# A fused attention and two-layer kernel: second layer's list by its places, conversions from slot 28 on, raw loads ahead of stores

## The chip, the cores and the metric

One core of one Trainium2 chip. The metric is device time in microseconds (us), the median of the timed runs. TensorE is called PE here, VectorE DVE, ScalarE ACT, GpSimd POOL, and SyncE, which issues all transfers of this kernel, SP.

## What is computed

Attention with a decay (no softmax) for 4 sequences of 576 tokens and 8 heads of 64, and then two feed-forward layers over the 2304 tokens. The weights come as 64-bit floats, which the chip must turn into pairs of 32-bit ones.

```python
def reference(q, k, v, moe_w_in, moe_w_out, moe2_w_in, moe2_w_out):
    # q, k, v: (4, 8, 576, 64); w_in: (512, 2048), w_out: (2048, 512), float64
    scores = q @ k.transpose(0, 1, 3, 2) / 8
    a = (scores * Dmat) @ v              # Dmat[h] = gamma_h ** (i - j) for i >= j, else 0
    x = a.transpose(0, 2, 1, 3).reshape(2304, 512)
    h = x @ moe_w_in
    x = (h * cos(h)) @ moe_w_out
    h = x @ moe2_w_in
    g = where(h >= 1, h, where(h <= -1, 0, (h + 1) ** 2 / 4))
    return g @ moe2_w_out
```

## The kernel before

**First layer.** Tokens go in five blocks (256 and then four times 512), the hidden units in 16 columns of 128. A *slot* is one block by one column; there are 80, those of blocks 0 and 1 mixed with each other (0 to 31), then 16 for each of blocks 2, 3 and 4. In slot s PE runs twelve matmuls `h<-xhl,wi` (L612) and the second twelve of slot s-2, `bky<-gh,wo` and `bky<-gl,wo` (L627 to L629). In between, h * cos(h) is made in turn by ACT (L662), DVE (L666), ACT (L670, L671), DVE (L675), ACT (`gh`, L683) and POOL (`gl`, L688): the high part `gh` and the low part `gl` of the result, since each matmul operand is kept as two parts. PE takes up the attention of a later block (L384) between slots, with steps on POOL (L370, L380), DVE (L472, L418, L519) and ACT.

The weight columns of block 0 and 1 are converted by these engines from the raw 64-bit words (loads `raw`, `rsh`), stored to `wd` and reloaded (`wi<-wd`, L314) three slots ahead of each use from block 2 on. Buffers for `wi` are a ring of five (pool `wr`).

**Background work.** The 32 matrices of the second layer (16 columns of each of two weights) are converted during the first layer. The list `bg` is spread over the slots from `bg0` to the sixth from the end. A matrix is loaded in its slot (`load_raw`, L200), begun one slot later (ACT, L226), and in the slot after that turned into 32-bit values on DVE (`W<-X` L239, `X<-W` L240, `X<-raw,X` L275, `V<-W,X` L276), split into parts `cw` (ACT L291, DVE L292) and stored (`wq<-cw`, `wv<-cw`, L294). With the second of a pair come sums and differences of the pair (DVE L300 to L302, parts `tw` on ACT L304, DVE L306, POOL L308, stores L310). `cw` takes its buffer from the ring of five of `wi`.

A scheduler sets the order of each engine from slot 24 on; ahead of that the opening's list does it.

**Second layer.** It computes its products in seven combinations of matrices each, over three token blocks of 768 and four steps of the hidden units: twelve units `n` of seven products (`bkT<-xc,w`, twelve matmuls each) and seven groups (`bkT<-gh,w`, `bkT<-gl,w`). Inputs are loaded from `yd` into four tiles `q` (`q<-yd`, four loads a token block), summed on DVE (`q<-q,q`), and split into `xc` parts 0 to 8 in turn (ACT rounds, DVE subtracts). Weights come in a ring of seven tiles `w`. Its steps are first written down as operations with an engine, a cost, a place in time `pos` and what they wait for; `listed()` then walks through them with a clock of its own and makes the order of each engine, which is kept as it is. The inputs of a later token block have places from 70 before it on, the weights 16 before their product; a unit has 28. Products 1, 6, 2, 5, 7, 4 and 3 of the first unit are mixed with the last two second halves of the first layer. Ahead of product 6 ACT copies bank T0 into T1 (`bkT1<-bkT0`, "the seed"), on which PE goes on adding up.

In `listed()` the time from which an operation may be placed was, for all, 60 ahead of the first product:

```python
ready = [-60.0] * len(ops)
free = dict(PE=0.0, ACT=-60.0, DVE=-60.0, POOL=-60.0, SP=-60.0)
```

Of the kernel before, what the change touches and what calls it, by code (L numbers as in the profile page):

```python
# [23 lines left out]
NC = DFF // P  # L24
# [86 lines left out]
def retention_moe_kernel(ctx: ExitStack, tc: tile.TileContext, qk, kv, win1, wout1, win2, wout2, ktab, out):  # L111
# [25 lines left out]
    V, A, G, SY, PE = [Ordered(e) for e in (nc.vector, nc.scalar, nc.gpsimd, nc.sync, nc.tensor)]  # L137
# [37 lines left out]
    def behind(later, earlier):  # L175
        tc.add_manual_dep(later.ins, earlier.ins.name, mybir.DependencyInfo(mybir.DependencyClass.NoSync, mybir.DependencyReason.SCHED_ONLY), reason="pace")
# [16 lines left out]
    def load_raw(L, i, c, homes=None):  # L193
        src = wsrc[L, i][c]
        twice = L == 0 and (i, c) not in ONCE
        tag = "raw" if twice else ("raw", "rsh")[turn[0] % 2] if L == 0 else ("raw", "raw", "rsh")[turn[0] % 3]
        turn[0] += not twice
        pool, first, second = (cv, tag, "rsh") if homes is None else (wp, *homes)
        t = pool.tile([P, DM, 2], I32, tag=first, name="raw")
        i0 = SY.dma_start(out=t, in_=src)  # L200
        if L == 1 and len(done) > 1:
            behind(i0, done[-2])
        t2 = None
        if twice:
            t2 = pool.tile([P, 4 * DM], I16, tag=second, name="rsh")
            SY.dma_start(out=t2[:, 1:], in_=src.rearrange("p n two -> p (n two)").bitcast(I16)[:, :4 * DM - 1])
        raws[L, i, c] = t, t2
# [47 lines left out]
    def begin(L, i, c, after=None):  # L255
        return Conversion(L, i, c, after).X()
# [3 lines left out]
    def home1(i, c):  # L260
        if i == 0:
            wi[0, c] = wr.tile([P, 2, DM], F32R, tag="wi", name="wi")
            return wi[0, c]
        wo[0, c] = wp.tile([P, 2, DM], F32R, tag=f"wo{c}", name=f"wo{c}")
        return wo[0, c]

    def store1(c):
        SY.dma_start(out=wd[c], in_=f(wi[0, c]))
# [43 lines left out]
    def load_wi(c):  # L312
        t = wr.tile([P, 2, DM], F32R, tag="wi", name="wi")
        SY.dma_start(out=f(t), in_=wd[c])  # L314
        wi[0, c] = t
# [283 lines left out]
    pos_of = {x: s for s, x in enumerate(slots)}  # L599
# [37 lines left out]
    def evac(s, home=None, only=None):  # L637
        l, c = slots[s]
        if c != NC - 1:
            return  # L640
        o, n = BLOCKS[l]
        per = 512 // n
        for e, y in enumerate(yb[l]):
            if only not in (None, e):
                continue
            t = stp.tile([P, 512], F32, tag="st", name="st") if home is None else home
            copy_out(e, t, y, -TWOPI)
            SY.dma_start(out=yd[:, e * per:(e + 1) * per, o:o + n], in_=t.rearrange("p (k n) -> p k n", k=per))
# [44 lines left out]
    def steps_of(s, which):  # L693
        for x in which:
            if (x, s) not in taken:
                taken.add((x, s))
                STEPS[x](s)
# [6 lines left out]
    def run_plan(pos):  # L704
        for fn in plan.pop(pos, []):
            fn()
# [141 lines left out]
    queue = [x for x in order if x not in loaded]  # L848
# [1 line left out]
        load_raw(0, *queue.pop(0))  # L850

    bg = [x for q in range(NQ) for x in ((0, q), (0, q + NQ), (1, q), (1, q + NQ))]
    bg0 = pos_of[1, NC - 1] + 2
    begun2 = {}
    per = (N1 - 6 - bg0) / len(bg)
    bgpos = {}
# [7 lines left out]
    def spill_2(i, c):  # L864
        spill(i, c, begun2.pop((i, c)))
        if c >= NQ:
            spill_sums(i, c - NQ)

    ops = []
# [99 lines left out]
    for s in range(N1):  # L969
        l, c = slots[s]  # L970
        if s == 24:
            by_hand[0] = 0
        run_plan(2 * s)
        steps_of(s, "m")
        if s >= 1:
            steps_of(s - 1, "CgG")
        steps_of(s, "haA")

        todo = [x for x in jobs.get(s, []) if x not in opened]
        begun = [begin(0, *x) for x in todo]  # L980
        for x in todo:
            begun.pop(0).rest(home1(*x))
            if x[0] == 0:
                store1(x[1])
            if queue:
                load_raw(0, *queue.pop(0))
        run_plan(2 * s + 1)
        if s >= LAG:
            steps_of(s - LAG, "M")
            evac(s - LAG)  # L990
        for x in bgpos.get(s - 2, []):
            spill_2(*x)
        for x in bgpos.get(s, []):
            load_raw(1, *x)
        steps_of(s, "b")
        for x in bgpos.get(s - 1, []):
            begun2[x] = begin(1, *x, after=mark[0])
        for c2 in reload.get(s, []):
            load_wi(c2)

        for fn in early.get(s, ()):
            fn()
# [217 lines left out]
    def listed():  # L1220
        waits = [len(o[4]) for o in ops]
        users = [[] for _ in ops]
        for n, o in enumerate(ops):
            for x, lands in o[4]:
                users[x].append((n, lands))
        ready = [-60.0] * len(ops)
        free = dict(PE=0.0, ACT=-60.0, DVE=-60.0, POOL=-60.0, SP=-60.0)
        queue = {e: {n for n, o in enumerate(ops) if o[0] == e and (e == "PE" or not waits[n])} for e in free}
        order = []
        while len(order) < len(ops):  # L1230
            best = None
            for e, ns in queue.items():
                if e == "PE":
                    n = min(ns, default=None)
                    if n is None or waits[n]:
                        continue
                elif ns:
                    t1 = min(max(free[e], ready[n]) for n in ns) + 0.15
                    n = min((n for n in ns if max(free[e], ready[n]) <= t1), key=lambda n: (ops[n][2], n))
                else:  # L1240
                    continue
                t = max(free[e], ready[n])
                if best is None or t < best[0]:
                    best = t, n
            t, n = best
            e, cost = ops[n][:2]
            queue[e].remove(n)
            free[e] = t + cost
            order.append((t, n))
            for u, lands in users[n]:  # L1250
                ready[u] = max(ready[u], t + cost + (0.0 if not lands or ops[u][0] == e else 6.0 if e == "SP" else 0.12))
                waits[u] -= 1
                if not waits[u] and ops[u][0] != "PE":
                    queue[ops[u][0]].add(u)
        return order

    order2 = listed()
    by_hand[0] = 1
    for _, n in order2:
# [103 lines left out]
```

## Time and profile before

| | |
|---|---|
| median of 3 timed runs | 835.67 us (834.68 to 838.59) |
| profiled execution | 838.97 us, span from first to last instruction 837.2 us |
| PE busy | 811.9 us, 97% |
| PE weight loads | 729.6 us, 87% |
| DVE busy | 642.5 us, 77% |
| ACT busy | 543.1 us, 65% |
| POOL busy | 166.9 us, 20% |
| granted PE clock, mean | 0.993 |
| moved by DMA | 232.92 MB, 278 GB/s |

Shares are of the span and average over stages with different limits: the first layer runs to about 470 us, the second from there to the end. A matmul's end is modelled, and matmuls overlap, so the distance from one start to the next says how fast PE goes. In a row of the timeline, "[4.81 <-ACT bkT L128]" is idle time of the engine ahead of that instruction and the step that ended it. L128 is the line of a helper that records whatever an ordered list issues; there the tile names tell the steps apart.

### The profile page before, as it was taken

The numbers are of one execution on the slowest core, as the hardware profiler recorded it, in microseconds if no ns is written. First come the engines' busy times: TensorE is split into PE (matmuls) and PEld (weight loads), VectorE is DVE, ScalarE is ACT, GpSimd is POOL, SyncE is SP. The second block draws the span as 40 slices with busy tenths as digits, with TensorE's granted clock in tenths as the row PEclk, the third lists the DMA queues.
The fourth block names the chain that finished last, engine by engine and source line by source line (L and its number), as shares of the span: only waits on it lengthen the run. The fifth ranks groups of instructions, "written<-read, shape, count | busy, mean of one in ns | idle before, by whom it ended". The sixth has DMA issues, their size and how long they took to land.

```text
span 837.2 us, 14788 instructions
## 1 busy us (share of the span) xinstructions
PE 811.9 (97%) x5549; PEld 729.6 (87%) x5550; DVE 642.5 (77%) x933; ACT 543.1 (65%) x893; POOL 166.9 (20%) x131
## 2 busy tenths in 40 slices
PE   8999899999999999999999799999999999999997
PEld 5788789888778677778777699999999999999997
DVE  7988878448898899888986548589786776874676
ACT  4778788754656554656666458678657786566672
POOL 2333223432334444234244100000000000000000
PEclk9999999999999999999999899999999999999999
DMA  9997999745888997687977478889897888898883
GB/s 351 379 386 267 352 326 324 263 154 182 300 299 312 328 340 293 237 278 278 362 286 252 151 276 250 253 255 322 255 327 253 254 251 254 263 319 250 256 253 136
DMA packets 78007, 232.92 MB, mean 278 GB/s; under 512 B 8304, under 2 KB 15088, under 8 KB 77936
## 3 DMA queue, kind: packets, MB, share of 16 engines
q1 hardware_dynamic: 77936, 231.98, 80.7%
q8 instruction: 44, 0.72, 0.3%
q14 instruction: 27, 0.22, 0.1%
HBM read 184.76 MB, written 47.19 MB: 277 GB/s over the span
## 4 chain that ended last, share of the span: by engine, by line
PE 43%; DVE 6%; DMA 3%; ACT 2%; issue 1%; SPq 0%; POOL 0%; DVEq 0%; ACTq 0%
PE bkT L128 41%; DMA wi<-wd 2%; DVE cw L292 1%; DVE t L666 1%; DVE X L275 1%; DMA wq<-cw 1%; DVE t L675 1%; DVE V L276 1%; DMA q<-yd 0%; PE bky L128 0%; DMA wv<-tw 0%; PE bky L629 0%; DMA wv<-cw 0%; PE bkO L612 0%; PE h L612 0%
## 5 line engine op out<-in xcount | busy, mean ns | idle before, releaser
L128 PE MATMUL bkT<-xc,w 128*128 128x384 f32 x1008 | 180.9, 337 | 4.8 <-ACT bkT L128 4.8
L128 PEld LDWEIGHTS bkT<-xc,w 128*128 128x128 f32 x1008 | 176.8, 189 | 5.6 <-ACT bkT L128 5.5
L128 PE MATMUL bkT<-gh,w 128*128 128x384 f32 x672 | 170.8, 335 | 0.3 <-ACT bkT L128 0.3
L612 PE MATMUL h<-xhl,wi 128*128 128x512 f32 (+1 forms) x576 | 139.3, 389 | 2.3 <-DVE t L675 2.3
L612 PEld LDWEIGHTS h<-xhl,wi 128*128 128x128 f32 x576 | 105.5, 188 | 26.1 <-DVE t L675 4.2
L128 PEld LDWEIGHTS bkT<-gh,w 128*128 128x128 f32 x672 | 121.2, 188 | 0.6 <-ACT bkT L128 0.6
L688 POOL TENSOR_TENSOR gl<-t,gh 128x512 fp32r<-128x512 f32 (+1 forms) x57 | 81.6, 1433 | 158.0 <-ACT gh L683 99.5
L128 PE MATMUL bkT<-gl,w 128*128 128x384 f32 x336 | 112.3, 334 | 0.0
L629 PE MATMUL bky<-gl,wo 128*128 128x512 f32 x208 | 78.6, 393 | 4.2 <-POOL gl L688 4.2
L627 PE MATMUL bky<-gh,wo 128*128 128x512 f32 x208 | 81.8, 394 | 0.0
L628 PE MATMUL bky<-gh,wo 128*128 128x512 f32 x208 | 81.1, 390 | 0.0
L683 ACT ACTIVATE gh<-t 128x512 fp32r<-128x512 f32 (+1 forms) x57 | 35.3, 619 | 53.9 <-DVE t L675 53.9
L128 PEld LDWEIGHTS bkT<-gl,w 128*128 128x128 f32 x336 | 63.1, 188 | 0.0
L128 DVE TENSOR_TENSOR gl<-a,gh 128x768 fp32r<-128x768 f32 x48 | 45.2, 953 | 14.0 <-ACT gh L128 14.0
L128 PE MATMUL h<-xhl,wi 128*128 128x256 f32 (+1 forms) x288 | 53.0, 335 | 2.7 <-ACT hs L128 2.7
L670 ACT ACTIVATE t<-t 128x512 f32<-128x512 f32 (+1 forms) x56 | 34.9, 623 | 31.3 <-DVE t L666 31.2
L128 DVE SCALAR_TENSOR_TENSOR a<-bkT,a 128x768 f32<-128x768 f32 x36 | 34.4, 956 | 26.2 <-ACT a L128 25.6
L128 PEld LDWEIGHTS h<-xhl,wi 128*128 128x128 f32 x288 | 44.6, 194 | 8.6 <-ACT hs L128 3.1
L629 PEld LDWEIGHTS bky<-gl,wo 128*128 128x128 f32 x208 | 38.8, 188 | 14.7 <-POOL gl L688 6.7
L128 DVE TENSOR_TENSOR a<-bkT,a 128x768 f32<-128x768 f32 (+1 forms) x46 | 43.0, 937 | 10.9 <-PE bkT L128 10.9
L627 PEld LDWEIGHTS bky<-gh,wo 128*128 128x128 f32 x208 | 39.0, 188 | 8.8 <-issue 0.5
L128 ACT ACTIVATE gh<-a 128x768 fp32r<-128x768 f32 x48 | 40.1, 836 | 8.8 <-PE bkT L128 8.4
(187 smaller groups left out, 1529.9 us busy)
## 6 DMA issues: line engine op xcount, KB each, us to landing
w<-wq SPq DMA_DIRECT2D x84, 512.0 KB, 4.5
w<-wv SPq DMA_DIRECT2D x84, 512.0 KB, 4.6
wi<-wd SPq DMA_DIRECT2D x48, 512.0 KB, 5.2
raw<-in_win_dram SPq DMA_DIRECT2D x32, 512.0 KB, 6.1
raw<-in_wout_dram SPq DMA_DIRECT2D x32, 512.0 KB, 5.4
qkv<-in_qk_dram SPq DMA_DIRECT2D x16, 512.0 KB, 7.0
qkv<-in_kv_dram SPq DMA_DIRECT2D x16, 512.0 KB, 8.5
wd<-wi SPq DMA_DIRECT2D x16, 512.0 KB, 6.3
```

Source lines behind the costliest of these rows:

```text
L128: ins = fn(*args, **kw)
L275: V.scalar_tensor_tensor(out=X, in0=raw[:, :, 0].bitcast(U32), scalar=2.0 ** -52, in1=X, op0=ALU.mult, op1=ALU.mult)
L276: done.append(V.tensor_tensor(out=v, in0=W, in1=X, op=ALU.add))
L292: V.tensor_tensor(out=t[:, ks, 1], in0=u, in1=f(t)[:, ks, 0], op=ALU.subtract)
L612: lastpe[0] = PE.matmul(hp[s][:, :n], w[:, a, kb, :], x[b][:, kb, :], start=(i == 0), stop=(i == 3 * KB - 1))
L627: PE.matmul(o, w[:, 0, es], a, start=first and e % per == 0, stop=False, skip_group_check=True)
L628: PE.matmul(o, w[:, 1, es], a, start=False, stop=False, skip_group_check=True)
L629: PE.matmul(o, w[:, 0, es], b, start=False, stop=last, skip_group_check=True)
L666: V.scalar_tensor_tensor(out=t, in0=t, scalar=-MAGIC, in1=h, op0=ALU.add, op1=ALU.subtract)
L670: A.activation(u, u, AF.Sin, scale=TWOPI / 2)
L683: A.activation(gh[s], rt[s], AF.Copy)
L688: G.tensor_tensor(out=gl[s], in0=u, in1=f(gh[s]), op=ALU.subtract)
```

## The change

Three edits. The background conversions begin at slot 28 (`pos_of[0, NC - 1] + 1`) instead of 33. In a slot that converts and stores a column of the first layer, the next raw loads are issued ahead of the stores. And in `listed()` an operation on SP, or one that waits for nothing, may be placed no earlier than its own `pos`; all others, and the engines PE, ACT, DVE and POOL, start at 0.

```diff
-    bg0 = pos_of[1, NC - 1] + 2
+    bg0 = pos_of[0, NC - 1] + 1
...
         for x in todo:
             begun.pop(0).rest(home1(*x))
+            if queue:
+                load_raw(0, *queue.pop(0))
+        for x in todo:
             if x[0] == 0:
                 store1(x[1])
-            if queue:
-                load_raw(0, *queue.pop(0))
...
-        ready = [-60.0] * len(ops)
-        free = dict(PE=0.0, ACT=-60.0, DVE=-60.0, POOL=-60.0, SP=-60.0)
+        ready = [o[2] if o[0] == "SP" or not o[4] else 0.0 for o in ops]
+        free = dict(PE=0.0, ACT=0.0, DVE=0.0, POOL=0.0, SP=-60.0)
```

In `ops`, `o[0]` is the engine, `o[2]` the place `pos` and `o[4]` the set of operations waited for.

ACT at the seam of the layers, from the last `gh` of the first layer on; xc5 and xc6 are inputs of the first token block, xc7 and xc8 of the second. Before:

```order
L683 ACTIVATE gh_5436<-t_5418 128x512
L128 ACTIVATE xc5_5483<-q2_4976 128x768
L128 ACTIVATE xc6_5498<-q3_4978 128x768
L128 ACTIVATE xc7_5481<-q0_4972 128x768
L128 ACTIVATE xc8_5482<-q4_5071 128x768
L128 ACTIVATE bkT1_5536<-bkT0_5511 128x2x384
L128 ACTIVATE u2_5480<-bkT1_5536 128x768
L128 ACTIVATE a1_5478<-bky0_4770 128x512
```

And now:

```order
L683 ACTIVATE gh_5436<-t_5418 128x512
L128 ACTIVATE bkT1_5518<-bkT0_5493 128x2x384
L128 ACTIVATE xc5_5534<-q2_4978 128x768
L128 ACTIVATE u2_5480<-bkT1_5518 128x768
L128 ACTIVATE xc6_5551<-q3_4980 128x768
L128 ACTIVATE a1_5478<-bky0_4793 128x512
```

The seed has moved ahead of the four roundings, and xc7 and xc8 have left this place.

DVE at the turn from blocks 0 and 1 to block 2, from the copy-out of block 0 (`st<-bkO`) on; `t<-t,hs` are the steps L666 and L675 of a slot of block 1. Before:

```order
L635 TENSOR_SCALAR st<-bkO 128x512
L666 SCALAR_TENSOR_TENSOR t<-t,hs 128x512
L675 SCALAR_TENSOR_TENSOR t<-t,hs 128x512
L666 SCALAR_TENSOR_TENSOR t<-t,hs 128x512
L675 SCALAR_TENSOR_TENSOR t<-t,hs 128x512
L666 SCALAR_TENSOR_TENSOR t<-t,hs 128x512
L675 SCALAR_TENSOR_TENSOR t<-t,hs 128x512
```

And now:

```order
L635 TENSOR_SCALAR st<-bkO 128x512
L666 SCALAR_TENSOR_TENSOR t<-t,hs 128x512
L239 TENSOR_SCALAR W<-X 128x512
L240 TENSOR_SCALAR X<-W 128x512
L275 SCALAR_TENSOR_TENSOR X<-raw,X 128x512
L675 SCALAR_TENSOR_TENSOR t<-t,hs 128x512
L276 TENSOR_TENSOR V<-W,X 128x512
L666 SCALAR_TENSOR_TENSOR t<-t,hs 128x512
L239 TENSOR_SCALAR W<-X 128x512
L240 TENSOR_SCALAR X<-W 128x512
L292 TENSOR_TENSOR cw<-V,cw 128x2x256
L275 SCALAR_TENSOR_TENSOR X<-raw,X 128x512
```

The steps of the conversions stand between L666 and L675 here already.

SP at the same turn, from the first reload `wi<-wd0` on; `wd0` to `wd4` are the columns that block 2 begins with. Before:

```order
L314 DMA wi_2306<-wd0_101 128x1024
L200 DMA raw_2670<-in_wout2_dram 128x1024
L364 DMA qkv_2246<-in_qk_dram 128x1024
L364 DMA qkv_2246<-in_kv_dram 128x1024
L314 DMA wi_2345<-wd1_102 128x1024
L314 DMA wi_2387<-wd2_103 128x1024
L364 DMA qkv_2347<-in_qk_dram 128x1024
L364 DMA qkv_2347<-in_kv_dram 128x1024
L648 DMA yd_100<-st_2298 128x2x256
L648 DMA yd_100<-st_2301 128x2x256
L314 DMA wi_2426<-wd3_104 128x1024
L314 DMA wi_2543<-wd4_105 128x1024
```

And now:

```order
L648 DMA yd_100<-st_2303 128x2x256
L314 DMA wi_2367<-wd1_102 128x1024
L294 DMA wq0_117<-cw_2355 128x512 x2
L200 DMA raw_2593<-in_win2_dram 128x1024
L314 DMA wi_2430<-wd2_103 128x1024
L294 DMA wq0_117<-cw_2411 128x512
L310 DMA wq0_117<-tw_2418 128x512 x4
L200 DMA raw_2476<-in_wout2_dram 128x1024
L294 DMA wv0_121<-cw_2472 128x512
L314 DMA wi_2480<-wd3_104 128x1024
L314 DMA wi_2600<-wd4_105 128x1024
```

The reloads of block 2 have spills and raw loads between them now, and `wd1` has moved behind both stores of block 0.

## Rows read from the trace of the kernel before

**Rows 1.** The page, part 1: busy time, share of the span, instructions.

```profile
PE 811.9 (97%) x5549; PEld 729.6 (87%) x5550; DVE 642.5 (77%) x933; ACT 543.1 (65%) x893; POOL 166.9 (20%) x131
```

**Rows 2.** Busy time by stage: stretch, length, engines, PE clock, DMA share, GB/s.

```profile
163.00:191.00 28.00, 28.00 (x223) 22.82 (x223) 12.82 (x22) 15.53 (x27) 9.17 (x7) 1.00 0.56 189
191.00:260.00 69.00, 68.83 (x585) 55.26 (x584) 59.60 (x104) 40.44 (x74) 24.68 (x20) 1.00 0.78 269
260.00:355.00 95.00, 92.00 (x767) 73.57 (x766) 85.46 (x135) 54.66 (x95) 36.91 (x26) 1.00 0.84 300
355.00:455.00 100.00, 95.40 (x412) 76.43 (x412) 86.78 (x126) 62.38 (x108) 37.81 (x25) 1.00 0.84 299
```

**Rows 3.** Timeline of PE at the seam: start, length, instruction, count, idle before.

```profile
469.35 2.24 PE L128 MATMUL bkT<-xc,w 128*128 128x384 f32 x12
471.43 0.62 PE L128 MATMUL bky<-gh,wo 128*128 128x512 f32 x2
...
473.93 0.39 PE L128 MATMUL bky<-gl,wo 128*128 128x512 f32 x1
479.13 4.21 PE L128 MATMUL bkT<-xc,w 128*128 128x384 f32 x12 [4.81 <-ACT bkT L128]
483.14 1.00 PE L128 MATMUL bky<-gh,wo 128*128 128x512 f32 x2
...
486.25 14.07 PE L128 MATMUL bkT<-xc,w 128*128 128x384 f32 x80
```

**Rows 4.** Busy time by stage, behind the seam and deep in layer two.

```profile
479.10:483.10 4.00, 3.97 (x12) 3.97 (x13) 2.10 (x3) 0.00 (x0) 0.00 (x0) 0.50 0.01 2
...
520.00:800.00 280.00, 280.00 (x1615) 280.00 (x1615) 202.15 (x224) 190.93 (x239) 0.00 (x0) 1.00 0.84 270
```

**Rows 5.** Timelines of ACT and DVE at the seam.

```profile
477.54 0.84 ACT L128 ACTIVATE xc<-q 128x768 fp32r<-128x768 f32 x1 [2.28 <-DVE q L128]
478.29 0.79 ACT L128 ACTIVATE bkT<-bkT 128x768 f32<-128x768 f32 x1
...
476.55 1.95 DVE L128 TENSOR_TENSOR q<-q,q 128x768 f32<-128x768 f32 x2 [2.51 <-DMA q<-yd]
```

**Rows 6.** Timeline of SP at the seam.

```profile
467.23 7.19 SPq L128 DMA_DIRECT2D q<-yd  x4
```

**Rows 7.** Timeline of PE, three of its ten idle times from 260 to 455.

```profile
278.56 0.50 PE L629 MATMUL bky<-gl,wo 128*128 128x512 f32 x1 [1.51 <-POOL gl L688]
...
372.54 3.04 PE L612 MATMUL h<-xhl,wi 128*128 128x512 f32 x12 [0.99 <-DVE t L675]
...
452.21 1.19 PE L629 MATMUL bky<-gl,wo 128*128 128x512 f32 x4 [0.75 <-POOL gl L688]
```

**Rows 8.** Groups of DVE by line and form, 190 to 460: busy, mean ns, idle.

```profile
L275 DVE SCALAR_TENSOR_TENSOR X<-raw,X 128x512 f32<-128x512 uint32 x32 | 25.7, 804 | 0.7
...
L301 DVE TENSOR_TENSOR V<-V 128x256 f32<-128x256 f32 x16 | 6.8, 423 | 0.5
```

**Rows 9.** Timeline of DVE, first step of a conversion.

```profile
191.40 1.49 DVE L239 TENSOR_SCALAR W<-X 128x512 int32<-128x512 int32 x1
```

**Rows 10.** Third token block's inputs: SP's timeline, busy time by stage.

```profile
563.19 0.37 SPq L128 DMA_DIRECT2D q<-yd  x1
...
570.00:580.00 10.00, 10.00 (x59) 10.00 (x59) 8.98 (x11) 8.21 (x11) 0.00 (x0) 1.00 1.01 379
```

**Rows 11.** Waits of SP's queue (us, times, longest), and landing of reloads.

```profile
SPq L294 <- DVE cw L292: 52.6, 21, 5.5
...
SPq L314 <- DMA wq<-cw: 14.3, 4, 7.0
...
wi<-wd SPq DMA_DIRECT2D x48, 512.0 KB, 5.2
```

**Rows 12.** POOL: timeline near the seam; group by form, 190 to 460.

```profile
466.23 1.29 POOL L688 TENSOR_TENSOR gl<-t,gh 128x512 fp32r<-128x512 f32 x1 [2.63 <-ACT gh L683]
...
L688 POOL TENSOR_TENSOR gl<-t,gh 128x512 fp32r<-128x512 f32 x43 | 64.3, 1497 | 122.9 <-ACT gh L683 78.3 <-issue 41.9 <-PE bky L629 1.9
```

## Prediction

> **What bounds the kernel now.** I read the busy line of the page first: PE is busy 811.9 of 837.2 us [rows 1], so whatever the other engines do, the time can fall only where PE stands still or runs at a lower clock. The busy time by stage then tells where that is. From 191 to 260 us PE loses 0.17 us in all; from 260 to 455 us it loses 3.00 + 4.60 = 7.60 us [rows 2]; from 520 to 800 us, deep in the second layer, nothing, at the full clock [rows 4]. Third, the timeline of PE around the seam between the layers: behind the matmul at 473.93 us it is idle for 4.81 us, released by ACT's `bkT` [rows 3]. So there are two sorts of loss: one hole at the seam, and ten small ones while the first layer's last blocks run, most of them put down to DVE's L675 or to POOL's `gl` behind it [rows 7]. The opening up to 100 us has losses too, but the two orders agree there row by row.
>
> The hole at the seam is read from three engines. ACT's step that PE waits for is the seed, a copy of bank T0 into T1, at 478.29 us; its input is there once the first product is through, a little after PE goes on to its next work at 471.43 us [rows 3]. It comes so late because ACT's row has four xc roundings ahead of it, and the last, at 477.54, waited 2.28 us for DVE's `q` at 476.55, which waited 2.51 us for a load q<-yd [rows 5]. That load is one of the four of the *second* token block, issued from 467.23 us on [rows 6]; PE needs nothing of them in the first four units of products.
>
> **The list of the second layer.** The new starting times keep a load from being planned before its place, and ACT and DVE from being planned before zero. In ACT's new order the seed comes first, with xc7 and xc8 more than forty rows further down; PE's order from the first product on is the same in both. What goes, start to start: the product behind the hole began at 479.13 and would begin when the twelve matmuls ahead of it end, 473.93 + 0.23 = 474.16: 4.97 us. Its own twelve matmuls took 483.14 - 479.13 = 4.01 us, where the first product's took 471.43 - 469.35 = 2.08: 1.93 us, and the twelve behind it 486.25 - 483.14 = 3.11 where the twelve from 471.43 took 474.16 - 471.43 = 2.73: 0.38 us [rows 3]. These two are the clock: granted 0.50 (1.2 of 2.4 GHz) from 479.1 to 483.1 us, after the engine had stood idle [rows 4]. Sum 4.97 + 1.93 + 0.38 = 7.28, **7.3 us**.
>
> What is late next? The seed can begin when the first product is done, by 471.7, takes 0.79 [rows 5] and ends at 472.5, 1.7 us before PE wants it. The four loads that stood ahead of the weights now stand behind 23 weight loads, whose ring of seven reaches 7 x 2.08 = 14.6 us ahead of PE. That loads do no harm there is seen on those of the third token block, which already lie between weight loads at 563.19 us: PE was busy 10.00 of the 10.00 us from 570, with the DMA engines full [rows 10]. So they cost nothing while the ring is full; without that cover one late weight, a product's length of 2 us. Bounds of the part: 7.6 to 5 us.
>
> **Conversions from slot 28 on.** 32 matrices are still converted, the last still from slot 72 on, so nothing is removed; 41 slots become 46 (1.28 and 1.44 slots a matrix). On DVE ten groups of steps do this, 162.6 us in all or 5.1 us a matrix, from 25.7 us (L275) down to 6.8 us (L301) [rows 8]. A slot is 24 matmuls of 0.227 us, 5.44 us; of these the conversions take 5.1 / 1.28 = 4.0 us now and 5.1 / 1.44 = 3.5 us then. DVE as a whole is busy 85.46 + 86.78 of 195 us, 88% [rows 2]; 0.5 us less in each slot makes it 79%. The new place has room: from 163 to 191 us DVE was busy 12.82 of 28 us and the DMA engines 56% [rows 2], and the first conversion began at 191.40 us [rows 9]; five slots earlier is 164. Five slots take 3.5 matrices, 18 us, and 12.82 + 18 = 31 is a little more than the 28 there are, so I don't count on this stretch staying without holes. At 59.60 of 69 us PE lost 0.17 us, between 191 and 260 [rows 2].
>
> What this saves is not in the rows, so I bound it. At best the holes shrink to what the stretch from 191 to 260 us shows, 0.17 in 69 or 0.5 in 195: a gain of 7. At worst the new stretch pays the 3 us that don't fit, the old holes stay, and as the order within a slot changes everywhere, one more of the largest kind comes in (1.51 us [rows 7]): a loss of 4.5. I take a gain of **2 us**, between the ends and nearer to no gain: with the trace's durations laid on DVE's order, twelve slots hold more than 5.44 us of steps between two L675 now and nine then, so a quarter of 7.6 should go.
>
> **Raw loads ahead of stores.** SP's order is the same row for row up to the first reloads of block 2, and all slots with such stores lie ahead of that. So the edit moves no instruction, **0 us** either way: not the text but the scheduler sets the place there. If a load did move, its cover would be the two raw tiles already filled.
>
> **Sum.** 7.3 + 2 + 0 = 9.3 us. Against the profiled execution, 838.97 us (span 837.2 and 1.8 around it), that is 829.7; it was 3.3 us over the median of the timed runs, 835.67, so for the median the forecast is **826.4 us**. With the bounds: 835.67 - 7.6 - 7 = 821.1 to 835.67 - 5 + 4.5 = 835.2, both ends unlikely together.
>
> **Rivals.** First, *the small holes stay or move forward*: the conversions press by their order in DVE's queue, not by their share of it. For it: a hole of 0.75 us came even at 452 us [rows 7], among the last conversions, whose place stays. Time 835.67 - 7.3 = 828.4, up to 832.9 with the loss of 4.5.
>
> Second, *the list does not do what it says*: the seed comes early but PE meets another late step right behind it, the banks that DVE and ACT empty for the fourth product, or a weight behind the stores of those banks. Against it: these steps follow PE's own matmuls, as they do now. If the whole hole only shifted: 835.67 - 2 = 833.7.
>
> Third, *POOL and DVE hold each other up in the moved slots*. POOL's `gl` takes 1.29 us where no conversion runs (466.23) and 1.50 in the mean among them [rows 12]. At worst DVE would stand for a whole `gl` in each moved slot, 5 x 1.3 = 6.5 us: 826.4 + 6.5 = 832.9. Against it stands the 0.17 us lost from 191 to 260, with the same instructions side by side. The Trainium skill's page "SBUF — State Buffer", section "SBUF: two separate sides", has a rule that speaks for this rival: VectorE operations with two SBUF inputs and GpSimd operations share a port pair, and the one that starts first holds it for its whole instruction. The longer mean agrees with it in direction; that PE lost almost nothing says that such a block stays inside the slack.
>
> Fourth, **slower than before**: the spills now stand in SP's queue between the first reloads of block 2, and their `cw` tiles come from the ring of five that the reloads use. SP has waited up to 5.5 us for DVE's `cw`, and a reload up to 7.0 us for a `cw` store to leave its buffer; a reload lands in 5.2 us [rows 11]. Together that is 17.7 us, against a lead of three slots, 16.3; beyond that PE stands still. Two holes like the one at the seam, 7.1 us each with the clock, make 826.4 + 14.2 = 840.6. Against it: after 191 us the same queue does this without a PE wait for a reload.
>
> **Chances.** Forecast 0.64 (822.5 to 828.4), small holes stay 0.18, list without effect 0.08, POOL against DVE 0.04, late reloads 0.06. About 0.5% (4.2 us, so 831.5 and 839.9) is what a measurement of this kernel can tell from no change. The first rival lies below 831.5 for two thirds, 0.12: faster 0.64 + 0.12 = 0.76, same 0.06 + 0.08 + 0.04 = 0.18, slower 0.06. The range that holds the forecast and these two thirds, and a part of the rest since the cases' own edges are soft, is 822 to 832.
>
> **What would show it.** In the profile after: no wait of PE for ACT's `bkT` at the first products, and a granted clock of 1.00 there; q<-yd loads of the second token block some 40 us into the layer; the first W of a conversion near 164 us; DVE around 80% busy from 260 to 455, and PE's idle time there at 5 to 6 us instead of 7.6. Wrong would be a new PE wait for `wi` near slot 32, new waits for POOL's `gl` from 163 to 200 us, or a hole further on in the first unit of the second layer.

## The result and the profile after

The changed kernel takes 826.85 us in the median of four runs (825.69 to 827.89), the one before 835.76 us in four (834.68 to 838.59): a ratio of 0.9888, with a 95% interval of 0.986 to 0.9915. The forecast was 826.4 us, within 822 to 832.

The page after, its span and the busy time of each engine, answers to [rows 1]:

```profile
span 823.9 us, 14770 instructions
...
PE 806.9 (98%) x5549; PEld 726.7 (88%) x5550; DVE 641.5 (78%) x933; ACT 542.3 (66%) x893; POOL 164.7 (20%) x131
```

The instruction counts are the same as before. PE's time without work falls from 837.2 - 811.9 = 25.3 to 823.9 - 806.9 = 17.0 us, and its busy time by 5.0 us with the same matmuls, which I put down to the clock and to modelled ends.

Busy time by stage after, to be laid beside [rows 2, 4] (stretch, length, then PE, PEld, DVE, ACT, POOL with counts, granted clock, DMA share, GB/s):

```profile
163.00:191.00 28.00, 28.00 (x224) 22.84 (x223) 23.88 (x41) 16.09 (x28) 7.50 (x5) 1.00 0.77 261
191.00:260.00 69.00, 64.60 (x564) 51.33 (x563) 57.26 (x98) 40.37 (x75) 25.47 (x21) 1.00 0.78 275
260.00:355.00 95.00, 93.95 (x777) 75.90 (x776) 80.39 (x129) 55.02 (x96) 37.08 (x28) 1.00 0.84 298
355.00:455.00 100.00, 98.10 (x430) 79.98 (x429) 82.53 (x117) 62.13 (x103) 35.34 (x23) 1.00 0.78 273
463.00:473.00 10.00, 10.00 (x52) 8.96 (x51) 3.42 (x5) 5.21 (x8) 1.29 (x1) 1.00 0.24 80
```

Two things are to be seen. At the seam (463 to 473 now) PE is busy throughout at a clock of 1.00. And the small losses have moved: 4.40 us from 191 to 260, where 0.17 were lost before, and 1.05 + 1.90 = 2.95 us from 260 to 455, where it was 7.60.

PE's timeline at the seam after, the answer to [rows 3]:

```profile
463.37 2.24 PE L128 MATMUL bkT<-xc,w 128*128 128x384 f32 x12
465.45 0.62 PE L128 MATMUL bky<-gh,wo 128*128 128x512 f32 x2
...
468.18 2.24 PE L128 MATMUL bkT<-xc,w 128*128 128x384 f32 x12
470.26 0.62 PE L128 MATMUL bky<-gh,wo 128*128 128x512 f32 x2
...
472.99 2.27 PE L128 MATMUL bkT<-xc,w 128*128 128x384 f32 x12
```

The 4.81 us of idle time are gone, and the second product takes 470.26 - 468.18 = 2.08 us like the first. From 465.45 to 472.99 it is 7.54 us; the same stretch before, from 471.43 to 486.25 [rows 3], is 14.82. The difference is 7.28 us.

ACT's timeline after: the seed begins right behind the first product, and the rounding of an input follows it ([rows 5] had it the other way round):

```profile
465.65 0.80 ACT L128 ACTIVATE bkT<-bkT 128x768 f32<-128x768 f32 x1 [0.70 <-PE bkT L128]
466.35 0.84 ACT L128 ACTIVATE xc<-q 128x768 fp32r<-128x768 f32 x1
```

SP's timeline after shows the first input of the second token block ([rows 6]), now 502.94 - 463.37 = 39.6 us behind the first product:

```profile
502.94 0.43 SPq L128 DMA_DIRECT2D q<-yd  x1
```

**The two profiled executions differ by more than the medians.** Their times are 838.97 and 825.69 us, 13.3 apart, the medians 8.9. The rest lies in the opening, where the engines' orders agree row by row. PE's timeline before, and below it after:

```profile
91.00 2.61 PE L128 MATMUL h<-xhl,wi 128*128 128x256 f32 x12 [2.39 <-ACT hs L128]
...
97.99 1.07 PE L128 MATMUL bky<-gl,wo 128*128 128x512 f32 x4
```

```profile
88.13 1.70 PE L128 MATMUL h<-xhl,wi 128*128 128x256 f32 x12 [0.91 <-ACT hs L128]
...
93.59 1.07 PE L128 MATMUL bky<-gl,wo 128*128 128x512 f32 x4
```

The four `bky<-gl` matmuls start 4.40 us apart. Among the runs below, all with the same opening, this mark lies anywhere from 94.09 to 98.17 us, so it is a spread from run to run and not the change. The longer wait for `hs` is one part of it (2.39 against 0.91 us), the clock another: it was granted at 0.50 from 91.4 to 94.8 us before, and at 1.00 there after. Times within the first layer are therefore compared from this mark on: to the first product of the second layer it is 371.36 us before (469.35 - 97.99) and 369.78 after (463.37 - 93.59), 1.6 us less.

### The profile page after: what moved, and what is told of

Same layout as the page of the kernel before. It is cut to its first block, busy times and chain, and to the rows that moved or that the text cites. A ratio compares the mean times of both kernels' runs of the same rounds, so it can differ in the third digit from the quotient of the medians.

```text
span 823.9 us, 14770 instructions
## 1 busy us (share of the span) xinstructions
PE 806.9 (98%) x5549; PEld 726.7 (88%) x5550; DVE 641.5 (78%) x933; ACT 542.3 (66%) x893; POOL 164.7 (20%) x131
## 4 chain that ended last, share of the span: by engine, by line
PE 45%; DVE 14%; DMA 4%; ACT 4%; issue 3%; POOL 0%; SPq 0%; DVEq 0%; ACTq 0%
PE bkT L128 42%; DVE cw L292 3%; DVE t L666 2%; DMA raw<-in_win_dram 1%; DVE t L675 1%; DVE X L275 1%; DVE V L276 1%; ACT tw L304 1%; DVE W L239 1%; ACT t L662 1%; DVE tw L306 1%; DVE X L240 1%; DMA wq<-cw 1%; ACT cw L291 1%; PE bky L128 1%
## 5 line engine op out<-in xcount | busy, mean ns | idle before, releaser
L128 PE MATMUL bkT<-xc,w 128*128 128x384 f32 x1008 | 179.0, 335 | 0.0
L688 POOL TENSOR_TENSOR gl<-t,gh 128x512 fp32r<-128x512 f32 (+1 forms) x57 | 79.3, 1391 | 161.7 <-ACT gh L683 106.0
```

Source lines behind the costliest of these rows:

```text
L128: ins = fn(*args, **kw)
L688: G.tensor_tensor(out=gl[s], in0=u, in1=f(gh[s]), op=ALU.subtract)
```

## The experiments

There are two questions. Is the hole at the seam gone because of ACT's order, and does it cost what the sum said? And do the conversions press on PE by their **share** of DVE's time, as the forecast assumed, or by their **place** in DVE's row, as the first rival said?

### The list alone

```diff
-        ready = [-60.0] * len(ops)
-        free = dict(PE=0.0, ACT=-60.0, DVE=-60.0, POOL=-60.0, SP=-60.0)
+        ready = [o[2] if o[0] == "SP" or not o[4] else 0.0 for o in ops]
+        free = dict(PE=0.0, ACT=0.0, DVE=0.0, POOL=0.0, SP=-60.0)
```

> The kernel before with the second layer's list alone changed. Theory (the hole at the seam and the low clock behind it are worth 7.3 us and the conversions' move some 1.6): 835.8 - 7.3 = 828.5 us, ratio 0.991; in the profile no wait of PE for ACT's bkT at the first products, 2.08 us for the product behind L0, and the holes from 260 to 455 us as before, 7 to 8 us. Rival (the two edits only work together, since a first layer without its earlier conversions reaches the seam with other steps late): 831 to 834 us.

Measured: 828.5 us, ratio 0.9906 [0.9882, 0.9931], and no idle time of PE at the seam. 7.3 us were forecast for this part; 0.94% of 835.94 is 7.9. The small holes of the first layer sum to 7.3 us, against 7.8 before.

### Each half of the list's edit

The loads' places alone:

```diff
-        ready = [-60.0] * len(ops)
+        ready = [o[2] if o[0] == "SP" else -60.0 for o in ops]
```

> The kernel before, and in the list only the loads on SP held back to their place; ACT, DVE and POOL may still be planned from -60 on. ACT's order then has xc5 and xc6 ahead of the seed, but xc7 and xc8 are gone from there. Theory (what counts is that no step that waits for the second block's loads stands ahead of the seed): 828.5 us, as with the whole list; the seed begins right behind xc6, some 2.1 us after the last gh, and PE does not wait. Rival (the seed must be first; two roundings ahead of it are too many): a hole of 0.5 to 1.5 us stays, 829 to 831 us.

The engines' clocks alone, with the loads as early as before:

```diff
-        ready = [-60.0] * len(ops)
-        free = dict(PE=0.0, ACT=-60.0, DVE=-60.0, POOL=-60.0, SP=-60.0)
+        ready = [o[2] if o[0] != "SP" and not o[4] else -60.0 if o[0] == "SP" else 0.0 for o in ops]
+        free = dict(PE=0.0, ACT=0.0, DVE=0.0, POOL=0.0, SP=-60.0)
```

> The kernel before, and in the list only the clocks of ACT, DVE and POOL set to start at 0; the second block's loads may still be planned from -60 on, so they are issued at the seam as before. ACT's order has the seed first, and xc7 and xc8 some eight rows behind it. Theory (only ACT's order counts): 828.5 us. Rival (the early loads do harm of their own, ahead of the weights in SP's queue or by xc7 and xc8 in the first unit): a hole of 1 to 4 us in the first unit, 830 to 833 us.

Measured: 829.73 us, 0.992 [0.9899, 0.9942], and 828.46 us, 0.9915 [0.9889, 0.9941]. The hole is gone in both. ACT's timeline with the loads alone held back shows why that half is enough:

```profile
468.67 1.56 ACT L128 ACTIVATE xc<-q 128x768 fp32r<-128x768 f32 x2
470.14 0.79 ACT L128 ACTIVATE bkT<-bkT 128x768 f32<-128x768 f32 x1
```

Two roundings still stand ahead of the seed, but they are those of the first token block, whose loads landed long before. The seed ends at 470.93, and PE takes up its product at 472.00 without a wait. So it takes a step whose *load* is late ahead of the seed to make the hole; neither the number of steps there nor the early loads themselves do it.

### The conversions' start alone

```diff
-    bg0 = pos_of[1, NC - 1] + 2
+    bg0 = pos_of[0, NC - 1] + 1
```

> The kernel before, and only the conversions begin at slot 28. Theory (by the profiles of before and after PE reaches the seam 1.6 us earlier once the difference of the openings is taken off): 834.2 us, ratio 0.998, with the hole of 4.8 us at the seam as before; the holes move forward, some 4 us of them from 191 to 225 us. Rival A (the prediction's share of DVE: a quarter of the small holes goes): 833.8 us with 5 to 6 us of small holes. Rival B (nothing gained, the profile's 1.6 is chance): 835.8 us.

Measured: 834.75 us beside 835.94, ratio 0.999 [0.9973, 1.0006]: about 1 us, not clear of none. The hole at the seam stays. PE's timeline and then ACT's:

```profile
474.60 3.92 PE L128 MATMUL bkT<-xc,w 128*128 128x384 f32 x12 [4.86 <-ACT bkT L128]
```

```profile
473.01 0.84 ACT L128 ACTIVATE xc<-q 128x768 fp32r<-128x768 f32 x1 [2.40 <-DVE q L128]
473.76 0.79 ACT L128 ACTIVATE bkT<-bkT 128x768 f32<-128x768 f32 x1
```

The small holes sum to 6.7 us, and five of the eight lie between 194 and 222 us, as in the changed kernel. They came with this edit, not with the list.

### The idle time and the clock, taken apart

To the kernel before, small matmuls are added between the second half and the product that waits for the seed. They write columns of a bank that nobody reads. PE is then busy in the hole, while ACT's order stays as it was. First 20 of them, then 36:

```diff
+                def second_half(j=j):
+                    steps_of(N1 - 2 + j, "M")
+                    for _ in range(0 if j else 20):
+                        PE.matmul(bk[0][:, 1, TH:], weights[0, 2]..., xat(2)[:, 0, 0, :P], start=False, stop=True, ...)
```

> The kernel before, with 20 extra matmuls on PE between the twelve of L0 and the product that waits for the seed; they write columns of a bank that nobody reads, and take PE from 474.2 to about 478. The seed still comes at 478.3. Theory (of the 7.3 us at the seam 2.3 are the low clock after the idle time): the hole's place is filled, the product behind it takes 2.1 us instead of 4.0 and the twelve after it 2.7 instead of 3.1, granted clock 1.00; 835.9 - 2.3 = 833.6 us. Rival (the clock there falls for another reason than idleness, or twenty small matmuls don't hold it): 4.0 us again, 835.9 us.

> As e5_warm, with 36 extra matmuls instead of 20, since those took 0.117 us each and left 2.86 us idle: 36 take 4.2 us, from 474.2 to 478.4. Theory (idleness is what lowers the clock): the idle time ahead of the product falls below 1.2 us, its twelve matmuls take 2.1 to 2.2 us and the next twelve 2.73, so the second block of the seam is over about 2.2 us earlier than before, 0.997. Rival (small matmuls don't hold the clock): 3.6 us for the product again.

Twenty were too few: 837.18 beside 837.02 us, ratio 1.0001 [0.9984, 1.0018]. PE's timeline, and then the busy time over the waiting product:

```profile
474.30 2.34 PE L128 MATMUL bkT<-xc,w 128*128 128x128 f32 x20
...
479.50 3.78 PE L128 MATMUL bkT<-xc,w 128*128 128x384 f32 x12 [2.86 <-ACT bkT L128]
```

```profile
479.40:483.10 3.70, 3.60 (x12) 3.60 (x13) 2.16 (x3) 0.05 (x1) 0.00 (x0) 0.57 0.00 0
```

They took 0.117 us each, where I had reckoned 0.19, so 2.86 us of idle time were left. The granted clock behind it was 0.57 in the mean of these 3.7 us: 0.50, the lower of its two levels, up to 482.6, and then the upper. With 36, the same two views:

```profile
473.91 4.13 PE L128 MATMUL bkT<-xc,w 128*128 128x128 f32 x36
...
479.06 2.34 PE L128 MATMUL bkT<-xc,w 128*128 128x384 f32 x12 [1.02 <-ACT bkT L128]
...
483.98 2.27 PE L128 MATMUL bkT<-xc,w 128*128 128x384 f32 x12
```

```profile
479.40:483.10 3.70, 3.70 (x21) 3.38 (x20) 2.02 (x3) 1.30 (x2) 0.00 (x0) 1.00 0.00 0
```

Now 1.02 us is left, the clock stays at 1.00, and from the product's start to 483.98 it takes 4.92 us, where before it took 486.25 - 479.13 = 7.12 [rows 3]. So the clock's part of the hole is 2.2 us, and the sum had 1.93 + 0.38 = 2.31. The time itself, 835.27 beside 835.67 us, 0.9985 [0.9967, 1.0003], is too coarse to show it by itself, but it does hold the 2.2 us (0.9974).

### Are the small holes DVE's at all?

The changed kernel without three of a conversion's DVE steps (`W<-X`, `X<-W`, `X<-raw,X`); the last adds X to itself:

```diff
-        begun.W(0)
-        raw, X, W = begun.raw, begun.x, begun.w
-        V.scalar_tensor_tensor(out=X, in0=raw[:, :, 0].bitcast(U32), scalar=2.0 ** -52, in1=X, op0=ALU.mult, op1=ALU.mult)
-        done.append(V.tensor_tensor(out=v, in0=W, in1=X, op=ALU.add))
+        done.append(V.tensor_tensor(out=v, in0=begun.x, in1=begun.x, op=ALU.add))
```

> The changed kernel without three of the four DVE steps by which a matrix becomes 32-bit (it leaves out W<-X, X<-W and X<-raw,X, some 65 us of DVE; the last step adds X to itself). Theory (the small holes come from conversion steps in DVE's queue): DVE below 65% busy from 191 to 455 us, holes from 191 to 455 us 1 to 2 us instead of 7.3, time 821 to 822 us. Rival (the holes belong to the attention's and the next layer's own steps): holes of 4 us or more, 823.5 us or more.

Measured: 821.37 us, 0.981 [0.9784, 0.9837]. Busy time by stage:

```profile
191.00:260.00 69.00, 69.00 (x587) 55.45 (x586) 40.70 (x76) 40.98 (x74) 23.13 (x20) 1.00 0.82 293
260.00:355.00 95.00, 95.00 (x776) 75.61 (x775) 58.32 (x98) 54.84 (x96) 35.01 (x28) 1.00 0.81 286
```

PE never waits there, nor from 355 to 455. So all 7.3 us of small holes come from these three steps in DVE's row, those put down to POOL's `gl`, ACT's `gh` or the attention's `R` too. By what they do it, this run doesn't say: it takes away their place in the row, their share of DVE's time and what DVE loses with them beside POOL, all at once. From the mark in the opening to the first product it is 362.32 us, 7.5 less than in the changed kernel. That is the most there is to win here.

### The start three slots later, and three earlier

```diff
-    bg0 = pos_of[0, NC - 1] + 1
+    bg0 = pos_of[0, NC - 1] + 4
```

> The changed kernel with the conversions from slot 31 on instead of 28 (43 slots). Theory of the share (each slot of room is worth 0.3 us, 1.5 us for five): 826.85 + 0.9 = 827.8 us. Theory of the order (what matters is which conversion steps fall in front of an attention step or L675 in the same slot, and that shifts with every start): off that line by 1 us or more to either side, and the holes from 163 to 455 us at other places, between 5 and 10 us in sum.

```diff
-    bg0 = pos_of[0, NC - 1] + 1
+    bg0 = pos_of[0, NC - 1] - 2
```

> The changed kernel with the conversions from slot 25 on (49 slots), while the last matrices of the first layer are still being converted. Theory of the share: 826.85 - 0.9 = 826.0 us. Theory of the order: off that line by 1 us or more. Rival on the other side (the slots 25 to 28 have DVE busy with the first layer's own conversions, and raw tiles are shared): new holes from 140 to 165 us and 828 us or more.

By share, slot 31 should lie between the list alone (slot 33, 0.9906) and the change (slot 28, 0.9888), and slot 25 a little below the change. Slot 31 gave 833.37 us, 0.9955 [0.994, 0.997], which is 5.6 us worse than the change and worse than slot 33 too; slot 25 gave 827.75, 0.9886 [0.9866, 0.9906], the same as the change, and this interval holds the 0.9 us less of the share as well. So it is slot 31 that the share can't explain. Its PE, in its worst place, and DVE there:

```profile
270.50 5.49 PE L612 MATMUL h<-xhl,wi 128*128 128x512 f32 x12 [3.46 <-DVE t L675]
```

```profile
265.54 0.68 DVE L666 SCALAR_TENSOR_TENSOR t<-t,h 128x512 f32<-128x512 f32 x1
...
269.16 0.68 DVE L276 TENSOR_TENSOR V<-W,X 128x512 f32<-128x512 f32 x1
269.76 0.68 DVE L675 SCALAR_TENSOR_TENSOR t<-t,h 128x512 f32<-128x512 f32 x1
```

No step is idle or stretched here: six conversion steps (L302, L239, L240, L275, L306, L276) simply stand between one L666 and the L675 of the slot, 4.2 us from start to start, and PE stands still for 3.46 us. But L666 itself was late. ACT's step L662, which it waits for, was done at 263.22, and L666 began at 265.54, behind three long conversion steps. These, and POOL's timeline at the same time:

```profile
260.68 1.60 DVE L276 TENSOR_TENSOR V<-W,X 128x512 f32<-128x512 f32 x1
262.31 1.67 DVE L300 TENSOR_TENSOR V<-V 128x512 f32<-128x512 f32 x1
263.91 1.26 DVE L292 TENSOR_TENSOR cw<-V,cw 128x256 fp32r<-128x256 f32 x1
```

```profile
260.45 1.28 POOL L370 TENSOR_TENSOR qkv<-qkv,qtb 128x512 f32<-128x512 f32 x1 [6.21 <-DMA qkv<-in_qk_dram]
261.69 1.75 POOL L688 TENSOR_TENSOR gl<-t,gh 128x512 fp32r<-128x512 f32 x1
263.40 1.49 POOL L380 TENSOR_TENSOR qkv<-qkv,ktb 128x512 f32<-128x512 f32 x1
```

L276 takes 0.68 us at 269.16, and L300 and this form of L292 take 0.69 and 0.41 us in the changed kernel (at 186.22 and 209.36). The three are some 2.7 us too long here, and L666 began 2.3 us behind its input. By these rows some 2.3 of the 3.46 us, an estimate, are DVE's loss beside POOL and the rest the row itself; no run takes the two apart. Then the clock comes on top, in the busy time right behind:

```profile
270.50:274.50 4.00, 4.00 (x9) 3.13 (x10) 3.93 (x6) 1.83 (x3) 1.28 (x1) 0.50 0.97 321
```

At 0.50 the twelve matmuls take 275.78 - 270.50 = 5.28 us where 12 x 0.227 = 2.72 are usual. This one hole cost 3.46 + 2.56 = 6.0 us, more than the whole difference of this kernel to the change. Slot 25 has its holes in other places again: eight from 167 to 217 us, none from 260 to 355, 7.9 us in all.

### DVE's work handed to POOL

If share counted, relieving DVE would help. Two ways of it, from the changed kernel: all low parts `tw` on POOL, and the addition `V<-W,X` on POOL.

```diff
-        if i == 0:
-            V.tensor_tensor(out=t[:, :, 1], in0=v, in1=f(t)[:, :, 0], op=ALU.subtract)
-        for j in (0, 2)[:2 * i]:
+        for j in (0, 2):
```

> The changed kernel with the low parts of the first matrix's sums (tw, DVE L306, 1.36 us eight times) on POOL, as the other matrix's are; 11 us less on DVE, some 23 us more on POOL. By the light kernel (65 us less on DVE took away all 7.3 us of small holes) in proportion: 1.2 us less, 825.6 us. Rival (POOL's gl now waits behind the sums, two of 1.3 us in a row): new holes for POOL gl, 828 us or more.

```diff
-        done.append(V.tensor_tensor(out=v, in0=W, in1=X, op=ALU.add))
+        done.append(G.tensor_tensor(out=v, in0=W, in1=X, op=ALU.add))
```

> The changed kernel with the add that ends a conversion (V<-W,X, DVE L276, 0.8 us 32 times) on POOL: 25 us less on DVE, some 45 us more on POOL. In proportion to the light kernel: holes of 4 to 5 us instead of 7.3, 824 us. Rival (the add is in the middle of the chain of a conversion, and on POOL it takes twice as long and makes gl wait): holes for POOL gl, 828 to 832 us.

Both missed: 832.8 us, 0.9959 [0.9942, 0.9976], and 833.12 us, 0.9976 [0.996, 0.9993], some 6 and 7 us worse than the change. These are the times of the rivals, but their holes, for POOL's `gl`, came only with the addition on POOL (3.7 us in four, where the change has one of 1.18); with the `tw` there they sum to 1.3 us. With the `tw` on POOL the largest hole is at 199 us; PE's, DVE's and POOL's timelines:

```profile
199.36 0.33 PE L382 MATMUL bkO<-qkv 64*64 64x128 f32 x2 [3.99 <-DVE xhl L517]
```

```profile
196.92 1.63 DVE L275 SCALAR_TENSOR_TENSOR X<-raw,X 128x512 f32<-128x512 uint32 x1
198.47 0.41 DVE L517 TENSOR_TENSOR xhl<-bkS,xhl 128x256 fp32r<-128x256 f32 x1
```

```profile
196.66 3.02 POOL L306 TENSOR_TENSOR tw<-V,tw 128x512 fp32r<-128x512 f32 x2 [1.45 <-ACT tw L304]
```

A DVE step that takes 0.69 us elsewhere took 1.63 here, begun inside the first POOL step. So DVE was not relieved by 11 us but by 2 (242.13 of 292 us from 163 to 455, against 244.07 after), and this run says little on the share. With the addition on POOL, DVE's group for the pair's sum, POOL's for the addition, and the wait between them:

```profile
L300 DVE TENSOR_TENSOR V<-V 128x512 f32<-128x512 f32 x15 | 22.5, 1503 | 12.8 <-POOL V L276 12.5
```

```profile
L276 POOL TENSOR_TENSOR V<-W,X 128x512 f32<-128x512 f32 x28 | 38.2, 1363 | 48.3 <-DVE X L275 40.3 <-ACT t L671 6.4 <-ACT xhl L512 1.6
```

Here DVE is less busy, 224.00 us, and PE's holes are larger, 9.9 us. L300 takes 1503 ns where it takes 920 after, and it stands in DVE's row for 12.5 us waiting for POOL, with everything behind it. Of the 6 to 7 us these kernels lose, the holes are 2.0 and 2.6; more is the clock (0.98 from 191 to 260 us in both, as it was granted at 0.50 from 200.6 to 203.9 and from 205.1 to 208.5), and a part I could not place.

### The same work, spread over two slots

The test of the order by itself: nothing taken away, but the steps of a conversion from the addition on come a slot later, and not ahead of that slot's L675.

```diff
-    def to_fp32(begun, v):
+    def parts_of(begun):
         begun.W(0)
-        raw, X, W = begun.raw, begun.x, begun.w
+        raw, X = begun.raw, begun.x
         V.scalar_tensor_tensor(out=X, ...)
-        done.append(V.tensor_tensor(out=v, in0=W, in1=X, op=ALU.add))
+
+    def to_fp32(begun, v):
+        done.append(V.tensor_tensor(out=v, in0=begun.w, in1=begun.x, op=ALU.add))
+        behind(done[-1], last_c[0])
...
-        for x in bgpos.get(s - 2, []):
+        for x in bgpos.get(s - 3, []):
             spill_2(*x)
+        for x in bgpos.get(s - 2, []):
+            parts_of(begun2[x])
```

> The changed kernel with each conversion laid out over two slots instead of one: W<-X, X<-W and X<-raw,X as now, and the add, cw and the sums one slot later and only behind that slot's L675. The same steps, the same start at slot 28, the same DVE work. In DVE's order the longest row of other steps between an L675 and the next L666 falls from 12 to 9, and between L666 and L675 from 6 to 5. Theory of the order: the holes from 163 to 455 us fall from 7.3 to 4 or 5 us, none above 1.2 us, ratio to before 0.985 (823.5 to 825 us). Theory of the share: 7 us of holes as now, ratio 0.989. Rival on the other side (conversions that stay longer hold their X and W tiles and the raw tile longer, so ACT and the raw loads wait): 828 us or more, with DVE waiting for ACT's X.

Measured: 827.26 us beside 837.34, ratio 0.9868 [0.9838, 0.9898]. DVE is as busy as after (243.1 and 244.1 of 292 us from 163 to 455), yet the small holes sum to 4.7 us instead of 7.3, as the theory of the order said. With the same steps, a new order moves them. But the theory also said that none is above 1.2 us, and one of 1.94 us is, at 221.20, ahead of the attention's `bkS<-R,qkv`. The busy time behind it:

```profile
221.20:225.20 4.00, 4.00 (x76) 3.53 (x77) 2.53 (x4) 1.77 (x3) 0.00 (x0) 0.59 0.17 61
```

Directly ahead of the `R` that PE waited for, a `cw` step of DVE took 1.49 us beside POOL's `gl`, where 0.41 is usual, and behind the hole the clock was granted at 0.50 up to 225.3. So 2.6 us less of holes make the way from the mark to the first product only 1.5 us shorter (368.32). The time is above the 823.5 to 825 us that were expected; its ratio, 0.2% below the change's, lies within that one's interval, so this is not shown to be the faster kernel.

## Why the prediction was right, and where it was not

**The list: right to its size.** 7.28 us were summed and 7.28 are gone at the place. The split holds as well: 2.2 us of clock by the run with 36 small matmuls, and 5 of idle time. The cause is what the chain of three engines said, shown by the two halves of the edit: whatever keeps ACT's seed from standing behind a step of the second block removes the whole hole. That loads between the weight loads do no harm held too; after the first product PE loses nothing until 809 us.

**The store edit: right at nothing.** With it alone, and without it in the changed kernel, each engine's order is the same row for row. It wasn't run for that reason. The run of the conversions' start alone, which lacks this edit, has the order of the changed kernel up to the seam.

**The conversions: about the right gain, by a reason that failed.** I took 2 us. The runs give 0.8 to 1.6: the change against the list alone is 0.9906 - 0.9888 = 0.18%, 1.5 us; the start alone 0.1%; the trace from the opening's mark 1.6. No time is clear of nothing by its interval. The traces say it better. In the six profiles of kernels that start at slot 33 (before, the three runs with the list's edit or a half of it, and the two with small matmuls) the way from the mark to the first product is 370.88 to 372.28 us, in the two that start at slot 28 (the change, and the start alone) it is 369.78 and 369.12: 2.2 us less in the mean, without overlap. So the 2 us were about right in size. The idle times account for 7.78 - 7.34 = 0.4 us of the 1.6 only, but they are counted from modelled ends. Counted from start to start, where PE's next matmul comes over 0.3 us behind the last, the time beyond 0.23 us sums to 14.0 us before and 12.5 after on this way. That is 1.5 us, so the gain does lie in the holes.

The step that failed is "a quarter of 7.6 should go". I drew it from DVE's steps laid out slot by slot (twelve slots over 5.44 us now, nine then) and from DVE's share, which was to fall from 88% to 79%; by my own terms, 5.1 / 1.28 - 5.1 / 1.44 = 0.44 us a slot, it should have been 80%. DVE fell to (80.39 + 82.53) / 195 = 83.5%, and PE's idle time there not to 5 to 6 us but to 2.95. In return 4.40 us came up from 191 to 260, where I had taken the 0.17 as a sign that such work is cheap there. It was cheap under the *old* order. Slots 31 and 25 and the two-slot version show what stands in its place: with little changed but the order, the holes move and their sum goes from 7.3 to 8.3, 7.9 and 4.7 us. PE feels which steps stand ahead of the one that it waits for, L675 or the attention's `R` and `xhl`, and how long these take beside POOL; a new start throws that anew everywhere. This was the first rival, and I had it at 0.18 with "stay or move forward"; its mechanism ("by their order in DVE's queue, not by their share of it") was nearer to the truth than mine, at a price near the forecast's. That the start at slot 28 came out on the better side is luck of that order: slot 31, by the same edit, gives 833.4.

Four of PE's eight small holes after, in its timeline:

```profile
196.96 3.01 PE L612 MATMUL h<-xhl,wi 128*128 128x512 f32 x12 [1.11 <-DVE t L675]
...
219.57 0.32 PE L384 MATMUL bkS<-R,qkv 64*64 64x128 f32 x1 [1.66 <-DVE R L472]
...
286.89 0.32 PE L384 MATMUL bkS<-R,qkv 64*64 64x128 f32 x1 [1.05 <-DVE R L472]
...
411.07 0.73 PE L629 MATMUL bky<-gl,wo 128*128 128x512 f32 x2 [1.18 <-POOL gl L688]
```

And what stood ahead of the first of them, in DVE's timeline:

```profile
192.92 1.21 DVE L239 TENSOR_SCALAR W<-X 128x512 int32<-128x512 int32 x1
194.17 1.41 DVE L240 TENSOR_SCALAR X<-W 128x512 int32<-128x512 int32 x1
195.61 0.69 DVE L275 SCALAR_TENSOR_TENSOR X<-raw,X 128x512 f32<-128x512 uint32 x1
196.22 0.68 DVE L675 SCALAR_TENSOR_TENSOR t<-t,h 128x512 f32<-128x512 f32 x1
```

**POOL against DVE: more than I gave it.** L239 and L240 take 1.21 and 1.41 us here beside POOL steps; where POOL stands still each takes 0.41 to 0.43. That is some 1.8 us more than they need, and the hole is 1.11. It is not this place alone. From 163 to 455 us 61 steps of DVE take over 0.08 us more than their form's usual time without POOL, 43 us in all, and each of them runs beside a POOL step; it is 43 us before as after, and 16 in the kernel without the three steps, which has no holes. Directly ahead of three of the eight holes (196.96, 219.57, 445.01) such steps are 1.8, 0.9 and 1.6 us too long. So the third rival's mechanism is at work throughout, and was so in the kernel before. A further loss of 6.5 us did not come of it with the change. A loss of that size came when work was moved to POOL, but only a part of it is placed; and whether the small holes would go if POOL's steps did, no run shows. The Trainium skill's "SBUF — State Buffer", section "SBUF: two separate sides", has a VectorE step with two SBUF inputs and a GpSimd step that reads SBUF lock each other out, for the whole instruction of the one that starts first; the 1.63 us of the run with `tw` on POOL agree with that, of a step with two such inputs that began 0.26 us behind POOL's.

**The late reloads didn't come.** In the changed kernel no hole of PE from 163 us on is released by a load, from 163 to 191 us it loses nothing, and none stands near slot 32 for `wi`. The run from slot 31 has one of 0.80 us for a reload, at 426.08.

**The number.** 9.3 us were summed and 8.9 measured. That the two profiled executions differ by 13.3 would have misled: 4.4 us of it are in the opening. The sum had allowed for the 3.3 us by which the profiled execution lay over the median.

## What to carry to other kernels

On an engine that works in order, ask of each critical step what stands ahead of it, and what *that* waits for: one step of later work planned too early, with a late load, cost 7.3 us here, and either of two small edits removed it whole. Price filler work by the place it takes ahead of a step that another engine waits for, and by what runs beside it there, not by its share of the engine alone; a stretch that is quiet under one order proves nothing for another. And count a hole of the matrix engine with what its clock loses behind it: 2.2 us on 4.8 idle, and 2.6 on 3.5.

## What the hardware showed that I had not expected

- Handing DVE's work to POOL made the kernel 6 to 7 us slower at a lower busy share of DVE. A DVE step of 0.69 us took 1.63 beside a POOL step, and the pair's sum 1503 ns in the mean instead of 920.
- From 163 to 455 us DVE lost 43 of its 244 busy us beside POOL: a conversion step of 0.41 or 0.69 us took up to 1.5 or 1.8 there, and none was stretched where POOL stood still.
- Matmuls of 128 columns took 0.115 to 0.117 us each, and 36 of them in the hole left the clock at 1.00 behind 1.02 us of idle time; behind 2.86, 4.81, 3.46 and, in the two-slot run, 1.94 us it was granted at 0.50. The length of one hole doesn't tell: behind 2.39 us in the opening before it was 0.50, behind 2.33 us there in the run with the list alone 1.00, and with the addition on POOL it fell to 0.50 behind holes of 0.94 and 0.75 us.
- The opening, with one and the same order, reaches the mark anywhere from 93.59 to 98.17 us. A single profile of this kernel can mislead by half of the gain that was looked for.
